# Attention and a bilinear feed-forward layer on one core: empty slots before the late units, wider 128-token steps, a longer run of three weight pieces

## The chip, the core and the metric

The kernel runs on one core of a Trainium2 chip. A core has five engines with an instruction queue each: TensorE (PE, matmuls, with weight loads that overlap them, PEld), VectorE (DVE), ScalarE (ACT), GpSimd (POOL) and SyncE (SP). Here nearly all DMA transfers are issued by SP. Each engine executes its queue in order and waits on semaphores for the others. PE writes to PSUM, which holds eight banks; DVE and ACT read it, POOL does not use it in this kernel. The metric is the device time of one execution in microseconds (us).

## The reference

```python
# q, k, v: (8 batches, 8 heads, 576 rows, 64), tau = 0.02
scores = q @ k.T / 8
thresh = max(scores, axis=-1) - tau
scores = where(scores >= thresh, scores, -1e9)
attn   = exp(scores - max(scores)); attn /= sum(attn) + 1e-9
x      = (attn @ v), heads put side by side        # (4608 tokens, 512)
out    = ((x @ w_a) * (x @ w_b)) @ w_out           # d_ff = 1536, out (4608, 512)
```

The three weight matrices come in as float64 and are turned to float32 on the chip, piece by piece.

## The kernel before, in words

**Units and slots.** Two heads make a pair; 8 batches of 4 pairs are 32 pairs. 576 rows of a head are four times 128 rows and a rest of 64. A unit `(p, u)` is 128 query rows of pair `p`: `u` = 0 to 3 are the full blocks, `u` = 4 (`NT`) joins the rests of two pairs. The list `units` holds 16 units of batch 0 without its rests, then 18 of each other batch, and at its end (from index `late` = 142) two late units for the rests of batch 0, written as pairs 32 and 34. One loop goes over slots `g`; slot `g` issues the scores of unit `g`, the transposes and the swap of unit `g - 1`, the way back of unit `g - 2` and the product with v of unit `g - 3` (`PV_LAG` = 3). Before, there are 144 units and 147 slots.

**The path of a unit.** PE makes the scores into two PSUM buffers (L400). DVE takes the maximum (L407), ACT the exponential (L428), DVE masks and sums (L431) and inverts the sums (L442, L444), ACT scales (L450). For the first units PE transposes the weights (L475, `turn_pe`). Later ones go a longer way: DVE transposes 32 by 32 blocks (L496, `turn_blocks`), SP writes them to DRAM (`swap<-tw`), and SP reads them back rearranged (`wT<-swap`, `turn_back`). Then PE multiplies with v (L540), ACT and DVE copy the result into an x tile (L547, L548), and POOL makes a second copy with the halves exchanged (L563).

**The feed-forward blocks.** 256 tokens form a block: two per batch, and two made of the rests. Layer 1 multiplies x by w_a and w_b and multiplies the two results; layer 2 multiplies by w_out. Most blocks use a scheme with seven products in place of eight (`sevens_of`, L708, with sums by POOL), with some plain steps between (`plain`, L782, evicted by ACT at L788 and by DVE at L790). Layer 2 is L839, or L885 for the very first block, which runs before the sums of w_out exist. The two blocks of batch 0 have all of layer 1 plain, and part of it in steps of 128 tokens: four of six column tiles of the first block, all six of the second. A step has a 128-column tile `f` of one weight group (two tiles make a group), a token range, and both matrices in turn, and each of these takes one PSUM buffer. There are four such buffers (`banks`) of two banks for scores, products and steps together.

**What sets the order.** The program order is written out by this Python loop, and each engine keeps it. `advance(cols)` issues feed-forward matmuls until `cols` columns are spent; a slot's share is `pace`, at most 0.1 of a block's 36864 columns plus a constant 576, and no more than what lets the backlog last to the next block's arrival (`arrivals`). `plain` yields without work while the weights that it needs are not yet converted (`state["converted"]`); the rest of that slot's share is then dropped. `make_room` moves a product to the middle of a step.

**Weights.** 36 pieces of 128x512 are loaded by SP (`load_weights`) and converted with two operations each on ACT (L300, L301), POOL (L307, L326) and DVE (L313, L321). `early[g]` says which pieces start in slot `g`; they end in slot `g + 1`. The slots 0 to 3 take two pieces, 4 to 9 three, 10 to 14 two.

**Transfers.** Late in the kernel transfers are not issued at once but posted in a list (`post`) and issued at a pace, each behind the matmul that PE had reached in program order (`pump`, `passed`). The moves of the swap go ahead of others posted lately. `flush` issues all up to a given one without pacing, just before it is needed. For the late units `last_loads` gives the slots that post the k, the query rests (`qt`, eight small transfers each) and the v, and `last_preps` the slots in which DVE transposes k and qt (`prep`, L366). After the last slot `state["over"]` is set, and the blocks that are left run on, with element-wise work on DVE in place of POOL.

Of the kernel before, what the change touches and what calls it, by code (L numbers as in the profile page):

```python
# [22 lines left out]
PV_LAG = 3  # L23
BY_PE = 8
# [12 lines left out]
SEVENS = 2  # L37
# [17 lines left out]
def kernel(  # L55
# [38 lines left out]
    nc = tc.nc  # L94
    B, H, S, D = q.shape
    P = 128
# [3 lines left out]
    HP = H // 2  # L100
# [655 lines left out]
    def ffn(xT, what):  # L756
# [6 lines left out]
        n = CH // P  # L763
        steps = [(f, 0, HALF) for f in range(NG * n)]
        if kind == "first":
            by = (2 if h == 0 else NG) * n
            steps = [(f, c, c + P) for c in (0, P) for f in range(by)] + steps[by:]
        def plain(steps):
            for f, c0, c1, both in steps:
                while (state["converted"] < 2 * HP * (f // n + 1)  # L770
                       or kind == "first" and rows_of[h] * P < c1):
                    yield 0, 0, 0
                fs = f % n * P
                ht = hs[f][:, :, c0:c1]
                for w in both:
                    pab = banks(c1 - c0, "pab")
                    for k in range(H):
                        for r in range(2):
                            rows = slice(r * D, (r + 1) * D)
                            moving = (x if k < HP else xs)[rows, k % HP, c0:c1]  # L780
                            for c in range(2):
                                nc.tensor.matmul(pab[c * D:(c + 1) * D, r],  # L782
                                                 w[rows, f // n, k, fs + c * D:fs + (c + 1) * D], moving,
                                                 start=(k == 0), stop=(k == H - 1))
                        if k < H - 1:
                            yield c1 - c0, (H - 1 - k) * (c1 - c0), H * (c1 - c0)
                    if w is wa_sb:
                        nc.scalar.copy(ht, pab)  # L788
                    else:
                        nc.vector.tensor_tensor(ht, ht, pab, op=ALU.mult)  # L790
                    yield c1 - c0, 0, 0

        both = wa_sb, wb_sb
        h_of = [work.tile([P, m * n, 2, HALF], FP32, tag=tag, bufs=1, name="h")
# [184 lines left out]
    arrivals = [BY_PE + HP + PV_LAG] + [g + PV_LAG + 1 for g, (i, u) in enumerate(units)  # L979
                                        if i >= HP and i % HP == HP - 1 and parts(i, u)] + [UNITS + PV_LAG]  # L980
    first = {i: g for g, (i, u) in enumerate(units) if u == 0}
    second = {i: g for g, (i, u) in enumerate(units) if u == 2}
# [22 lines left out]

    n = 0
    for g in range(NPIECES):
        size = min(3 if 4 <= g < 10 else 2, NPIECES - n)
        early[g] = list(range(n, n + size))
        n += size  # L1010
    for g in range(len(units) + PV_LAG):
# [2 lines left out]
        while bulk and bulk[0][1] < g - 1:  # L1014
            pump()
        state["converted"] = state["added"]
        here = g < len(units)
        converting = bool(early.get(g)) or bool(early.get(g - 1))
        back = ()
        if BY_PE + 1 < g <= len(units) + 1:  # L1020
            n = g - PV_LAG
            back = (1 if 2 * BY_PE <= n and parts(*units[n]) else 0,)
            if not back[0]:
                turn_back(*units[g - 2])
        if here:
            i, u = units[g]
# [20 lines left out]
        if g > BY_PE and g <= len(units):  # L1047
            turn_blocks(*units[g - 1])
        if g > BY_PE:
            advance(PORTIONS[0] * pace)  # L1050
# [18 lines left out]
        if g > BY_PE:  # L1069
            n = g - PV_LAG  # L1070
            held = 0.0
            now = parts(*units[n]) if BY_PE <= n < len(units) else []
# [17 lines left out]
            if back and back[0] > 0:  # L1090
                turn_back(*units[g - 2])
        for n in early.get(g, [])[:1]:
            convert_first(n)
# [90 lines left out]
```

## Time and profile before

| | |
|---|---|
| median of 3 runs | 1459.63 us (1456.23 to 1460.97) |
| the profiled execution | 1453.36 us, span 1451.6 us |
| mean granted clock of PE | 0.994 |
| chain that ended last | PE 82%, DVE 7%, DMA 4%, issue 3%, SP's queue 2% |
| PE busy in the first slices of 36 us | 6, 7, 7, 8, 8, 8 tenths, then mostly 9 or more |

The profile is of one execution. A row of a timeline gives start, duration, engine, line, operation, output<-input, the number of instructions merged into it, and in brackets how long the engine was idle before it and what it waited for. "issue" means that the engine waited for nothing that the profile can name. Ends of matmuls are modelled, so a PE that is busy is not PE at its peak. A releaser that had long been done when the wait ended was not the real one; often a transfer was. Slots can be told from the starts of the scores (L400): slot 5 starts at 44.3 us, 10 at 96.5, 15 at 148.1, 18 at 175.8; the scores of the first late unit start at 1269.3 us.

### The profile page before, as it was taken

The numbers are of one execution on the slowest core, as the hardware profiler recorded it, in microseconds if no ns is written. First come the engines' busy times: TensorE is split into PE (matmuls) and PEld (weight loads), VectorE is DVE, ScalarE is ACT, GpSimd is POOL, SyncE is SP. The second block draws the span as 40 slices with busy tenths as digits, with TensorE's granted clock in tenths as the row PEclk, the third lists the DMA queues.
The fourth block names the chain that finished last, engine by engine and source line by source line (L and its number), as shares of the span: only waits on it lengthen the run. The fifth ranks groups of instructions, "written<-read, shape, count | busy, mean of one in ns | idle before, by whom it ended". The sixth has DMA issues, their size and how long they took to land.

```text
span 1451.6 us, 79189 instructions
## 1 busy us (share of the span) xinstructions
PE 1377.2 (95%) x35264; PEld 1240.9 (85%) x35264; DVE 1015.7 (70%) x2207; ACT 680.8 (47%) x1254; POOL 488.8 (34%) x685
## 2 busy tenths in 40 slices
PE   6778889999999999999999999999999999889998
PEld 4678588988988898989898899799988789789998
DVE  6897876887767877787778675777677777653223
ACT  5775544545455544545454544454545454421110
POOL 2673462424060606051513251424233242306000
PEclk9999999999999999999999999999999999999999
DMA  9976665667657765667566755577556765651000
GB/s 208 240 212 172 167 171 141 162 171 196 176 148 178 181 177 148 179 169 212 152 166 169 188 138 133 147 183 195 152 135 171 188 167 132 177 142 43 4 18 17
DMA packets 338531, 225.87 MB, mean 156 GB/s; under 512 B 182544, under 2 KB 321808, under 8 KB 338192
## 3 DMA queue, kind: packets, MB, share of 16 engines
q1 hardware_dynamic: 335680, 220.23, 59.4%
q8 instruction: 277, 4.54, 1.4%
q10 hardware_dynamic: 2512, 0.59, 0.2%
q14 instruction: 62, 0.51, 0.1%
HBM read 131.07 MB, written 89.65 MB: 152 GB/s over the span
## 4 chain that ended last, share of the span: by engine, by line
PE 82%; DVE 7%; DMA 4%; issue 3%; SPq 2%; ACT 1%; POOL 0%; DVEq 0%; ACTq 0%; POOLq 0%
PE pab L708 26%; PE po L839 20%; PE pab L782 18%; PE pv L540 9%; PE sc L400 9%; DVE mx L407 1%; DVE tw L496 1%; SPq L144 1%; DMA sums_u<-in_k_dram 1%; DVE tw L431 1%; DMA raw<-in_moe_w_a_dram 1%; DMA raw<-in_moe_w_b_dram 0%; SPq L157 0%; DVE low L313 0%; DVE thr L408 0%
## 5 line engine op out<-in xcount | busy, mean ns | idle before, releaser
L450 ACT ACTIVATE tw<-tw,rcp 128x576 f32<-128x576 f32 x272 | 196.1, 768 | 231.2 <-DVE rcp L444 231.2
L407 DVE TENSOR_REDUCE mx<-sc 128x1 f32<-128x576 f32 x288 | 204.4, 750 | 133.5 <-PE sc L400 133.0
L428 ACT ACTIVATE tw<-sc,bias,scalars 128x576 f32<-128x576 f32 x288 | 239.3, 831 | 10.3 <-ACT bias L427 0.2
L674 POOL TENSOR_TENSOR h<-h,u 128x512 f32<-128x512 f32 x28 | 35.1, 1274 | 597.1 <-DVE h L751 387.3
L431 DVE SCALAR_TENSOR_TENSOR tw<-sc,thr,tw 128x576 f32<-128x576 f32 x288 | 220.9, 798 | 9.5 <-ACT tw L428 9.3
L839 PE MATMUL po<-wo_sb,h 64*64 64x256 f32 x3264 | 206.7, 376 | 0.5 <-DVE h L751 0.3
L496 DVE STREAM_TRANSPOSE tw<-tw 128x576 f32<-128x576 f32 x272 | 194.3, 752 | 0.0
L400 PE MATMUL sc<-kT,qT 64*64 64x288 f32 x2048 | 172.9, 407 | 7.8 <-DVE sums L442 5.3
L839 PEld LDWEIGHTS po<-wo_sb,h 64*64 64x64 f32 x3264 | 156.3, 133 | 27.0 <-issue 1.1
L540 PEld LDWEIGHTS pv<-wT,vm 64*64 64x64 f32 x5472 | 162.0, 137 | 19.2 <-issue 13.7
L540 PE MATMUL pv<-wT,vm 64*64 64x160 f32 (+3 forms) x5472 | 171.4, 270 | 6.5 <-issue 6.0
L808 POOL TENSOR_TENSOR h<-h 128x256 f32<-128x256 f32 x177 | 123.9, 732 | 119.7 <-PE po L839 115.1
L839 PE MATMUL po<-sums_u,h 64*64 64x256 f32 x2448 | 151.3, 377 | 2.8 <-DVE h L790 2.8
L839 PEld LDWEIGHTS po<-sums_u,h 64*64 64x64 f32 x2448 | 112.7, 133 | 27.1 <-DVE h L790 5.8
L708 PE MATMUL pab<-xU,wb_sb 64*64 64x128 f32 x4096 | 135.2, 270 | 0.0
L708 PEld LDWEIGHTS pab<-xU,wb_sb 64*64 64x64 f32 x4096 | 130.3, 133 | 1.9
L400 PEld LDWEIGHTS sc<-kT,qT 64*64 64x64 f32 x2048 | 103.8, 133 | 32.2 <-DVE sums L442 5.8
L427 ACT ACTIVATE bias<-mx,scalars 128x1 f32<-128x1 f32 x288 | 82.8, 288 | 65.2 <-DVE mx L407 64.9
L547 ACT COPY xT<-pv 128x128 f32<-128x128 f32 (+1 forms) x72 | 18.2, 253 | 192.6 <-PE pv L540 192.6
L782 PE MATMUL pab<-xS,wb_sb 64*64 64x256 f32 (+1 forms) x1728 | 99.2, 337 | 4.4 <-issue 4.4
L548 DVE COPY xT<-pv 64x128 f32<-64x128 f32 (+1 forms) x144 | 39.4, 274 | 89.3 <-PE pv L540 87.7
L782 PE MATMUL pab<-xS,wa_sb 64*64 64x256 f32 (+1 forms) x1728 | 100.2, 337 | 0.0
(138 smaller groups left out, 2385.1 us busy)
## 6 DMA issues: line engine op xcount, KB each, us to landing
wT<-swap SPq DMA_DIRECT2D x244, 288.0 KB, 3.9
swap<-tw SPq DMA_DIRECT2D x480, 144.0 KB, 3.2
vm<-in_v_dram SPq DMA_DIRECT2D x144, 72.0 KB, 2.5
kT<-in_k_dram SPq DMA_DIRECT2D x128, 72.0 KB, 3.3
swap<-tw SPq DMA_DIRECT2D x128, 72.0 KB, 2.9
wT<-swap SPq DMA_DIRECT2D x56, 144.0 KB, 3.3
out_dram<-kept SPq DMA_DIRECT2D x30, 256.0 KB, 3.6
qT<-in_q_dram SPq DMA_DIRECT2D x112, 40.0 KB, 3.1
```

The lines of the kernel that those rows point to most:

```text
L400: nc.tensor.matmul(sc[m][o * D:(o + 1) * D, c], qT[r, q0:q0 + D], kT[r, c * SH:(c + 1) * SH], start=True, stop=True)
L407: nc.vector.tensor_reduce(mx[:, c], sc[j], axis=AX.XY, op=ALU.max)
L427: nc.scalar.activation(bias[:, j:j + 1], mx[:, j:j + 1], AF.Copy, scale=e_nscale)
L428: nc.scalar.activation(wb[j], sb[j], AF.Exp, bias=bias[:, j:j + 1], scale=e_scale)
L431: nc.vector.scalar_tensor_tensor(out=wv, in0=sb[j], scalar=thr[:, j:j + 1], in1=wv, op0=ALU.is_ge, op1=ALU.mult, accum_out=sums[:, j:j + 1])
L450: nc.scalar.activation(w, w, AF.Copy, scale=rcp[:, j:j + 1])
L496: nc.vector.transpose(w, w)
L540: nc.tensor.matmul(pv[c * D:(c + 1) * D, y], vm[rows, s], wT[y](rows, s), start=(s == 0), stop=(s == NSLOT - 1))
L708: nc.tensor.matmul(out[c * D:(c + 1) * D, r, f * P:(f + 1) * P], w[g][k][rows, w0:w0 + D], moving[k][rows], start=(fresh and k == 0 and f ...
L782: nc.tensor.matmul(pab[c * D:(c + 1) * D, r], w[rows, f // n, k, fs + c * D:fs + (c + 1) * D], moving, start=(k == 0), stop=(k == H - 1))
L808: (nc.vector if state["over"] else nc.gpsimd).tensor_tensor(*a, **kw)
L839: nc.tensor.matmul(po[c * D:(c + 1) * D, r, y], ht[rows, t0:t0 + D], other[rows, f], start=(f == 0), stop=(f == NF // 2 - 1))
```

## The change

There are three parts.

*Empty slots and moved transfers.* Each of the two late units gets an empty slot before it (`None` in `units`), in which no scores, swap or product are issued for a unit; the code that looks at a unit skips it. There are 146 entries and 149 slots. The table of late loads and preparations is shifted: k 0 and 1 are still loaded in slot `late - 4` but transposed one slot later; qt 0 is still loaded in `late - 2` and transposed one later; k 2 and 3 one later; qt 2 is loaded one slot later and transposed two later; v 0 is loaded one slot earlier, v 3 one later.

*Column tiles.* In the steps of 128 tokens both column tiles of a group are done in one step and share a PSUM buffer: for each matrix, tile `f` fills columns 0 to 127 of both banks and tile `f + 1` columns 128 to 255. Only the first matmul of the first tile starts the accumulation. One eviction then takes both tiles. Steps of 256 tokens are as before.

*Weights.* Slots 4 to 12 take three pieces, slot 13 the last one.

```diff
-            by = (2 if h == 0 else NG) * n
-            steps = [(f, c, c + P) for c in (0, P) for f in range(by)] + steps[by:]
+            by = 2 if h == 0 else NG
+            steps = [(f, c, c + P) for c in (0, P) for f in range(0, by * n, n)] + steps[by * n:]
...
-                fs = f % n * P
-                ht = hs[f][:, :, c0:c1]
+                m, cn = HALF // (c1 - c0), c1 - c0
+                late_f = f - (NG - SEVENS) * n
+                ht = h_of[1][:, late_f:late_f + m] if late_f >= 0 else h_of[0][:, f:f + m]
+                ht = ht[:, :, :, c0:c1].rearrange("p f r w -> p r f w")
                 for w in both:
-                    pab = banks(c1 - c0, "pab")
...
+                    pab = banks(m * cn, "pab").rearrange("p r (f w) -> p r f w", f=m)
+                    left = whole = m * H * cn
+                    for fm in range(m):
+                        fs = (f + fm) % n * P
+                        for k in range(H):
...
+                                    nc.tensor.matmul(pab[c * D:(c + 1) * D, r, fm],
+                                                     w[rows, f // n, k, fs + c * D:fs + (c + 1) * D], moving,
+                                                     start=(fm == 0 and k == 0), stop=(fm == m - 1 and k == H - 1),
+                                                     skip_group_check=m > 1)
+                            left -= cn
+                            if left:
+                                yield cn, left, whole
...
-    units += [(p, NT) for p in range(NPR, NPR + HP, 2)]
-    UNITS = len(units)
...
+    for p in range(NPR, NPR + HP, 2):
+        units += [None, (p, NT)]
...
-    last_loads = {late - 4: [("k", 0), ("k", 1)], late - 2: [("k", 2), ("qt", 0)], late - 1: [("k", 3), ("qt", 2)],
-                  late: [("v", 0), ("v", 1)], late + 1: [("v", 2)], late + 2: [("v", 3)]}
-    last_preps = {late - 2: [("k", 0), ("k", 1)], late - 1: [("qt", 0)], late: [("k", 2), ("k", 3), ("qt", 2)]}
+    last_loads = {late - 4: [("k", 0), ("k", 1)], late - 2: [("k", 2), ("qt", 0)], late - 1: [("k", 3), ("v", 0)],
+                  late: [("v", 1), ("qt", 2)], late + 1: [("v", 2)], late + 3: [("v", 3)]}
+    last_preps = {late - 1: [("k", 0), ("k", 1)], late: [("qt", 0)], late + 1: [("k", 2), ("k", 3)], late + 2: [("qt", 2)]}
...
-        size = min(3 if 4 <= g < 10 else 2, NPIECES - n)
+        size = min(3 if 4 <= g < 13 else 2, NPIECES - n)
...
-        here = g < len(units)
+        here = g < len(units) and units[g] is not None
...
-            back = (1 if 2 * BY_PE <= n and parts(*units[n]) else 0,)
-            if not back[0]:
+            back = (1 if 2 * BY_PE <= n and units[n] and parts(*units[n]) else 0,)
+            if not back[0] and units[g - 2]:
                 turn_back(*units[g - 2])
```

More of the change, by code (lines that the diff above doesn't have):

```diff
@@ L772, in plain @@
                     yield 0, 0, 0
-                fs = f % n * P
-                ht = hs[f][:, :, c0:c1]
+                m, cn = HALF // (c1 - c0), c1 - c0
+                late_f = f - (NG - SEVENS) * n
+                ht = h_of[1][:, late_f:late_f + m] if late_f >= 0 else h_of[0][:, f:f + m]
+                ht = ht[:, :, :, c0:c1].rearrange("p f r w -> p r f w")
                 for w in both:
-                    pab = banks(c1 - c0, "pab")
[L777 to L786, printed above, removed]
+                    pab = banks(m * cn, "pab").rearrange("p r (f w) -> p r f w", f=m)
[3 more added lines that the diff above has]
+                        for k in range(H):
+                            for r in range(2):
+                                rows = slice(r * D, (r + 1) * D)
+                                moving = (x if k < HP else xs)[rows, k % HP, c0:c1]
+                                for c in range(2):
+                                    nc.tensor.matmul(pab[c * D:(c + 1) * D, r, fm],
[5 more added lines that the diff above has]
+                                yield cn, left, whole
                     if w is wa_sb:
@@ L790, in plain @@
                         nc.vector.tensor_tensor(ht, ht, pab, op=ALU.mult)
-                    yield c1 - c0, 0, 0
+                    yield cn, 0, 0
         both = wa_sb, wb_sb
@@ L976 @@
     late = len(units)
[L977 to L985 removed]
+    for p in range(NPR, NPR + HP, 2):
+        units += [None, (p, NT)]
+    taken_by = [(g, *unit) for g, unit in enumerate(units) if unit]
+    arrivals = [BY_PE + HP + PV_LAG] + [g + PV_LAG + 1 for g, i, u in taken_by
+                                        if i >= HP and i % HP == HP - 1 and parts(i, u)] + [len(units) + PV_LAG]
+    first = {i: g for g, i, u in taken_by if u == 0}
+    second = {i: g for g, i, u in taken_by if u == 2}
+    last_loads = {late - 4: [("k", 0), ("k", 1)], late - 2: [("k", 2), ("qt", 0)], late - 1: [("k", 3), ("v", 0)],
+                  late: [("v", 1), ("qt", 2)], late + 1: [("v", 2)], late + 3: [("v", 3)]}
+    last_preps = {late - 1: [("k", 0), ("k", 1)], late: [("qt", 0)], late + 1: [("k", 2), ("k", 3)], late + 2: [("qt", 2)]}
     prep_copy(*prep_pe(0, "q"))
@@ L1046 @@
         load_weights(RAWS if g < 6 else RAWS - 1)
-        if g > BY_PE and g <= len(units):
+        if g > BY_PE and g <= len(units) and units[g - 1]:
             turn_blocks(*units[g - 1])
@@ L1071 @@
             held = 0.0
-            now = parts(*units[n]) if BY_PE <= n < len(units) else []
+            now = parts(*units[n]) if BY_PE <= n < len(units) and units[n] else []
             alone = units[n] if BY_PE <= n < 2 * BY_PE else None
@@ L1089 @@
                 running["owed"] -= NSLOT * width(p, h) // 2
-            if back and back[0] > 0:
+            if back and back[0] > 0 and units[g - 2]:
                 turn_back(*units[g - 2])
```

## The prediction

> **What bounds the kernel now.** First the page's busy rows, then a table of stretches that I cut at the stages, to see where TensorE (PE) is not busy.
>
> ```profile
> span 1451.6 us, 79189 instructions
> PE 1377.2 (95%) x35264; PEld 1240.9 (85%) x35264; DVE 1015.7 (70%) x2207; ACT 680.8 (47%) x1254; POOL 488.8 (34%) x685
> ...
> 150.00:174.00 24.00, 20.46 (x338) 9.84 (x337) 20.64 (x43) 12.51 (x25) 11.32 (x13) 0.93 0.74 183
> 174.00:238.00 64.00, 57.70 (x1919) 53.36 (x1912) 45.18 (x97) 29.13 (x58) 26.00 (x16) 1.00 0.62 157
> 238.00:1258.00 1020.00, 1005.13 (x25623) 905.31 (x25623) 762.29 (x1669) 507.87 (x915) 347.95 (x518) 1.00 0.65 167
> 1258.00:1271.00 13.00, 7.15 (x142) 5.58 (x135) 4.23 (x10) 3.55 (x7) 0.00 (x0) 0.92 0.60 147
> 1271.00:1320.00 49.00, 44.03 (x1272) 42.29 (x1268) 21.57 (x50) 11.29 (x25) 6.56 (x8) 0.95 0.46 122
> 1320.00:1447.00 127.00, 125.76 (x3208) 124.33 (x3198) 41.62 (x76) 14.34 (x23) 20.72 (x36) 1.00 0.04 12
> ```
>
> A stretch's row gives its length, the busy time of PE, weight loads, DVE, ACT and POOL, then the granted clock, the DMA share and GB/s. From 238 to 1258 us PE idles 15 us in 1020: the order of its work is fixed and it is the bound. After 1320 it only drains a backlog. What can be won lies before 238 us and in 1258 to 1320 (11 us idle, clock below 1). A stall of PE in either place moves the end by its full length, since the same matmuls follow it. Next the timeline of PE and DVE there:
>
> ```profile
> 1247.64 1.17 PE L400 MATMUL sc<-kT,qT 64*64 64x288 f32 x15
> ...
> 1269.30 2.48 PE L400 MATMUL sc<-kT,qT 64*64 64x288 f32 x15 [5.33 <-DVE sums L442]
> 1271.45 4.09 PE L708 MATMUL pab<-xU,wb_sb 64*64 64x128 f32 x124
> 1282.99 3.51 PE L708 MATMUL pab<-xU,wb_sb 64*64 64x128 f32 x117
> 1306.50 3.81 PE L540 MATMUL pv<-wT,vm 64*64 64x32 f32 x142 [3.66 <-issue]
> 1317.05 2.33 PE L540 MATMUL pv<-wT,vm 64*64 64x32 f32 x142
> ```
> ```profile
> 1268.93 0.31 DVE L366 STREAM_TRANSPOSE qT<-qT 128x128 f32<-128x128 f32 x1 [7.23 <-DMA qT<-in_q_dram]
> ```
>
> The scores of the first late unit (pair 32, the left-over rows of batch 0) waited 5.33 us. DVE sat 7.23 us in front of the transpose of their queries, whose eight transfers SP issued only at 1259.1 and 1265.6. The product of that unit then waited 3.66 us with no named releaser; SP issued its two transfers wT<-swap at 1303.35, so I read it as that round trip. After each wait the same groups run slower (2.48 against 1.17 us, 3.81 against 2.33). In the head:
>
> ```profile
> 149.48 0.74 PE L885 MATMUL po<-wo_sb,h 64*64 64x512 f32 x4
> 152.55 1.86 PE L885 MATMUL po<-wo_sb,h 64*64 64x512 f32 x8 [2.33 <-POOL wo_sb L326]
> 154.17 2.14 PE L540 MATMUL pv<-wT,vm 64*64 64x64 f32 x72
> 164.58 1.23 PE L540 MATMUL pv<-wT,vm 64*64 64x64 f32 x72
> ```
> ```profile
> PE pab L782 <- DVE h L790: 4.3, 4, 1.6
> PE po L885 <- POOL wo_sb L326: 3.4, 2, 2.3
> PE pab L782 <- DVE tw L431: 0.5, 1, 0.5
> ```
>
> The second fence is who PE waited for in 120 to 240 us (total, times, longest): second-layer matmuls waited for weights still being converted, and first-layer matmuls in 128-token steps waited for a PSUM buffer that DVE had not emptied.
>
> **Part 1, the empty slots and the moved transfers.** No matmul is added or removed. Each empty slot holds only feed-forward columns: about 3686 + 576 columns, and 256 columns of L782 cost 0.43 us (64 matmuls of one step, 2048 columns, in 3.45 us), so about 7.2 us per slot that are taken off the final drain (127 us), no new time. Removed, if the waits go: 5.33 + 3.66; and of the slow groups after them: scores 2.48 - 1.17 = 1.31; L708 4.09 - 3.51 x 124/117 = 0.37; product 3.81 - 2.33 = 1.48. Sum 12.15.
> Moved: the transposes of k 0 and 1 go from slot 140 to 141, of qt 0 from 141 to 142, of k 2 and 3 to 143, of qt 2 from 142 to 144. On SP, qt 2 (8 transfers) goes from slot 141 to 142, v 0 (4) from 142 to 141, v 3 (4) from 144 to 145; the rest keep their slot. qt 0 keeps its load slot and its place behind the eight swap and wT issues, so I let it land at 1268.9 again. Its reader now comes after an empty slot: PE was through slot 141 at 1264.0, plus 7.2 is 1271.2, 2.3 us after landing. Behind that transpose on DVE stand the copies of a product and an eviction (L790); PE has four PSUM pairs and product 7 before it needs them, so I cost this wait at nothing; without that cover it is the 2 to 5 us by which DVE is held. The next thing late is qt 2: after 1267.4 SP still has 32 issues (swap 4, wT 6, out 2, k 4, v 8, qt 8) of 0.45 to 0.65 us, ready at 1282 to 1288 plus 1.9 landing, and its scores start at 1264.0 + 7.2 + 8.2 + 7.2 = 1286.6. New stall between 0 and 3.3; I take 1.5, the middle, as pacing on PE can push either way. The late product gets its wT request at the start of a slot instead of its middle, and a slot and a half instead of one: nothing left. Of the last layers more is issued before the loop ends, so some of the 27 additions L808 that DVE does now (455 ns) go to POOL (732 ns): 7.5 us of POOL at most, and PE waited for L808 nowhere in the whole run, so nothing; without that cover, 7.5. Bounds of the part: -12.15 and, if the qt 2 wait repeats the old one with its slow groups (7.0) and the product waits again (5.1), 0. Taken: -10.65.
> [...]
>
> **Part 2, three pieces a slot to slot 12.** The 36 weight pieces end with slot 13 instead of 14, their last adds (L326) in slot 14 instead of 15. Slot 15 (148.1 to 156.4 us) could do only two F steps of layer 2 before it ran out of pieces, and waited. Removed: 2.33 + 1.10 us; slow groups after: product 2.14 - 1.23 = 0.91, the next scores 1.69 us for 13 against 1.15 for 16, so 0.7. Sum 5.0; I keep 0.5 of it, taken -4.5. Bounds 0 and -5.0. Added in slots 10 to 12: per piece DVE 0.68 + 0.42, ACT 0.68 + 0.68, POOL 0.61 + 1.28. From 120 to 150 PE is busy 29.97 of 30, which hides it; without the cover three pieces of 1.1 us on DVE, 3.3. Taken +1. The loads on SP stay: all 36 were issued by 110.5, with the conversions before slot 10 as they were.
> [...]
>
> **Part 3, both column tiles in one step.** Twenty evictions on ACT and twenty on DVE become ten and ten of twice the size:
>
> ```profile
> L790 DVE TENSOR_TENSOR h<-h,pab 128x512 f32<-128x512 f32 x34 | 22.9, 673 | 34.9 <-PE pab L782 34.9
> L790 DVE TENSOR_TENSOR h<-h,pab 128x256 f32<-128x256 f32 x20 | 8.0, 399 | 5.6 <-PE pab L782 5.5
> L788 ACT COPY h<-pab 128x256 f32<-128x256 f32 x20 | 7.3, 367 | 21.8 <-PE pab L782 21.7
> ```
>
> DVE 8.0 - 10 x 0.673 = 1.3 us less, ACT 7.3 - 10 x 0.58 = 1.5 less, both beside PE: nothing. What counts is that a PSUM pair now takes 3.5 us of matmuls instead of 1.75 before PE needs another, so DVE may be late by twice as much. The waits of L782 for a buffer from 101 to 235 us are 0.43, 0.56, 1.16, 0.49, 1.61 and 0.99, 5.24 together; the longest DVE delay there (scores ready at 177, eviction at 181.3) is 4.3 us, which one step plus the rest of the open one covers. Taken -4.0, bounds 0 and -5.24. Against it: an open group holds one of four pairs over the scores, product and transposes of slots 5 to 10. Waits of that kind now: transposes for the copy L548, 0.35 to 1.51; L782 for a score buffer, 0.92 to 1.45. Between 0 and 6 x 1.5 = 9; taken +1.5, as groups already stay open over slot ends before.
>
> **Sum.** -10.65 - 4.5 + 1 - 4.0 + 1.5 = -16.65. The profiled execution took 1453.36 us (span 1451.6 and 1.76 around it), 6.3 below the median of the runs, 1459.63. It would become 1436.7; from the median, which the result is compared with, 1443.0. I say 1443.
>
> **The rivals.** *The tail's waits come back in another place*: the issues behind qt 2 speak for it, the 2.3 us in hand against it; then only the head is left, -6.0: 1453.6. *The head gives nothing*: DVE is busy 9.75 of 10 us around 44 to 54 us and near 8 later, so a PE that waits less may wait elsewhere: 1459.6 - 10.65, 1449. *No change*: both at once, 1459. *Slower*: DVE executes in order, and qt 0, k 3 and qt 2 each block it behind SP's full queue. Each costs a wait like the old (7.0), 21 in all, and the product 5.1: 26.1 against 12.15 now, less 6.0 from the head: 1467.6. It decides once new stalls in the tail exceed 18.2 us. For it: SP issues almost without a gap from 1251.7 to 1278.7; against it: two empty slots give it 14 us more.
>
> **How the numbers follow.** Chances: forecast 0.52 (1435 to 1450), tail lost 0.15, head lost 0.13, no change 0.08, slower 0.12. A measurement of this kernel tells 0.3%, 4.4 us, from nothing. Below 1455.2 lie the forecast, the head-lost case and most of the tail-lost one: 0.76; within 0.3% 0.12; slower 0.12. The range runs from all bounds at their best (12.15 + 5.0 + 5.24 and the 2.8 of evictions, 1434.4) to no change, leaving out the slower case and a little below: 1435 to 1460.
>
> **What would show it.** Right: no wait of scores over 2 us after 1255; the product of the first late unit without a wait; no L885 wait for L326; L782 waits for L790 under 1.2 us before 240; PE's busy time unchanged. Wrong: a DVE wait for qT or kT of 5 us or more with PE stopped beside it, transposes L475 waiting over 1.5 us in slots 5 to 8, or these stalls gone and a span that stays.

## The result, and the profile after

| | median | range | ratio to the kernel before, 95% interval |
|---|---|---|---|
| before | 1457.28 us | 1456.12 to 1460.97 | |
| changed | 1448.15 us | 1446.29 to 1450.88 | 0.9933 [0.9914, 0.9952] |

The change makes the kernel faster by 0.67%, 9.8 us of 1457 by the ratio. The forecast was 1443.0 us. The profiled execution of the changed kernel has a span of 1446.4 us and a time of 1448.15, which is the median itself; that of the kernel before was a short one, 1453.36 against its median of 1457.28. So the two spans differ by only 5.2 us, and stages have to be compared over more kernels than two. All times here are medians; one disturbed execution of 3663.58 us, of the version that the table of stages calls "to 11, loads", is left out. The changed kernel's page, the lines that answer to those shown of before:

```profile
span 1446.4 us, 79185 instructions
...
PE 1380.9 (95%) x35264; PEld 1250.0 (86%) x35264; DVE 1006.6 (70%) x2188; ACT 680.2 (47%) x1243; POOL 496.1 (34%) x695
...
q8 instruction: 278, 4.55, 1.3%
```

PE's work is the same 35264 matmuls. (The last line is needed later.) The table of stretches of the changed kernel, cut as before; columns are the stretch, its length, busy time of PE, weight loads, DVE, ACT and POOL, the granted clock, the DMA share and GB/s:

```profile
120.00:150.00 30.00, 27.27 (x531) 20.14 (x526) 27.70 (x55) 16.77 (x35) 17.61 (x20) 0.94 0.47 112
150.00:174.00 24.00, 23.70 (x548) 19.30 (x544) 18.72 (x40) 12.54 (x23) 8.74 (x10) 1.00 0.81 203
...
1258.00:1271.00 13.00, 12.79 (x354) 10.90 (x350) 7.12 (x14) 5.46 (x9) 0.00 (x0) 1.00 0.52 117
1271.00:1320.00 49.00, 45.95 (x1106) 42.87 (x1102) 20.57 (x46) 10.00 (x21) 15.46 (x25) 0.97 0.51 133
1320.00:1442.00 122.00, 118.94 (x3179) 117.79 (x3171) 35.77 (x70) 14.12 (x24) 17.97 (x30) 1.00 0.04 12
```

In 150 to 174 us PE is busy 23.70 us, before 20.46. In 1258 to 1271 it is busy 12.79, before 7.15. But 120 to 150, where it was busy 29.97, has become 27.27 at a clock of 0.94. The timeline of the tail shows PE's stops there, then DVE's:

```profile
1273.05 0.90 PE L400 MATMUL sc<-kT,qT 64*64 64x288 f32 x4 [0.16 <-issue]
1274.18 1.04 PE L400 MATMUL sc<-kT,qT 64*64 64x288 f32 x10 [0.23 <-issue]
...
1287.74 2.53 PE L540 MATMUL pv<-wT,vm 64*64 64x160 f32 x67 [0.25 <-DMA wT<-swap]
...
1293.14 2.12 PE L400 MATMUL sc<-kT,qT 64*64 64x288 f32 x14 [2.08 <-issue]
...
1309.15 2.31 PE L540 MATMUL pv<-wT,vm 64*64 64x32 f32 x137
```
```profile
1272.64 0.31 DVE L366 STREAM_TRANSPOSE qT<-qT 128x128 f32<-128x128 f32 x1 [6.64 <-DMA qT<-in_q_dram]
...
1292.72 0.31 DVE L366 STREAM_TRANSPOSE qT<-qT 128x128 f32<-128x128 f32 x1 [7.52 <-DMA vm<-in_v_dram]
```

DVE sits in front of the query transposes, for 6.64 and 7.52 us. (The second row names a v transfer; SP issued the eight transfers of qt 2 from 1285.25 to 1290.13.) Before, the first of these waits was 7.23 us, and the second was short:

```profile
1278.43 0.31 DVE L366 STREAM_TRANSPOSE qT<-qT 128x128 f32<-128x128 f32 x1 [0.91 <-DMA qT<-in_q_dram]
```

But the scores of the first late unit are held by only 0.16 and 0.23 us (5.33 before), since an empty slot's work lies in front of them. The second late unit's scores do wait, 2.08 us, and run slowly after it. The product of the first late unit (1309.15) has no wait; before it had 3.66.

### The profile page after: what moved, and what is told of

It reads as the page before. It is cut to its first block, busy times and chain, and to the rows that moved or that the text cites. A ratio compares the mean times of both kernels' runs of the same rounds, so it can differ in the third digit from the quotient of the medians.

```text
span 1446.4 us, 79185 instructions
## 1 busy us (share of the span) xinstructions
PE 1380.9 (95%) x35264; PEld 1250.0 (86%) x35264; DVE 1006.6 (70%) x2188; ACT 680.2 (47%) x1243; POOL 496.1 (34%) x695
## 3 DMA queue, kind: packets, MB, share of 16 engines
q8 instruction: 278, 4.55, 1.3%
## 4 chain that ended last, share of the span: by engine, by line
PE 82%; DMA 7%; DVE 6%; issue 3%; SPq 2%; ACT 1%; DVEq 0%; ACTq 0%
PE pab L708 25%; PE po L846 19%; PE pab L787 18%; PE pv L540 9%; PE sc L400 9%; PE po L892 1%; DMA qT<-in_q_dram 1%; DVE mx L407 1%; DMA raw<-in_moe_w_a_dram 1%; DVE tw L496 1%; DMA sums_u<-in_moe_w_a_dram 1%; DVE tw L431 1%; DMA wT<-swap 1%; DMA swap<-tw 1%; DMA sums_u<-in_k_dram 1%
## 5 line engine op out<-in xcount | busy, mean ns | idle before, releaser
L431 DVE SCALAR_TENSOR_TENSOR tw<-sc,thr,tw 128x576 f32<-128x576 f32 x288 | 220.9, 798 | 9.8 <-ACT tw L428 9.5
L400 PE MATMUL sc<-kT,qT 64*64 64x288 f32 x2048 | 177.8, 407 | 6.6 <-issue 2.9
L400 PEld LDWEIGHTS sc<-kT,qT 64*64 64x64 f32 x2048 | 107.1, 133 | 31.4 <-issue 7.9
L787 PE MATMUL pab<-xT,wa_sb 64*64 64x256 f32 (+1 forms) x1600 | 93.1, 337 | 8.7 <-issue 4.6
```

The source lines that it names most:

```text
L400: nc.tensor.matmul(sc[m][o * D:(o + 1) * D, c], qT[r, q0:q0 + D], kT[r, c * SH:(c + 1) * SH], start=True, stop=True)
L431: nc.vector.scalar_tensor_tensor(out=wv, in0=sb[j], scalar=thr[:, j:j + 1], in1=wv, op0=ALU.is_ge, op1=ALU.mult, accum_out=sums[:, j:j + 1])
L787: nc.tensor.matmul(pab[c * D:(c + 1) * D, r, fm], w[rows, f // n, k, fs + c * D:fs + (c + 1) * D], moving, start=(fm == 0 and k == 0), sto ...
```

## The experiments

All ratios are to the kernel before on the same chip. Four versions, marked with an asterisk below, were measured on another chip than the other experiments, so versions are compared by their ratios. A ratio less 1, times 1457, gives the us quoted. Durations by stage come from fourteen profiles of thirteen kernels (part 2 alone was measured twice). I take a slot's start from its first scores matmul and cut the span at the starts of slots 12, 15, 46 and 141. Between slots 46 and 141 all of them execute the same program.

```
parts / kernel           span   slot 12 at  12-14  15-45  46-140  141-end
none                    1451.6     122.7    25.4   269.7   836.9   196.9
3                       1460.7     124.5    25.9   268.5   841.5   200.3
2                       1458.5     126.3    30.4   267.7   836.8   197.3
2 (second measurement)* 1453.1     118.4    30.9   265.1   841.1   197.6
2+3                     1451.7     121.6    30.2   263.4   837.9   198.6
1                       1443.7     118.5    26.1   269.6   839.8   189.7
1+2*                    1449.8     124.6    31.0   267.4   837.4   189.4
1+3                     1449.4     116.6    25.6   268.4   848.7   190.0
1+2+3, the change       1446.4     116.8    31.1   263.4   844.0   191.1
 qt ahead               1444.8     119.8    30.2   265.8   837.9   191.0
 pieces to 11           1445.0     123.8    29.3   263.2   839.9   188.9
 to 11, loads           1450.7     124.6    30.8   265.8   842.3   187.2
 to 11, loads, order*   1433.5     120.4    27.6   263.4   836.7   185.3
1+3, loads*             1438.6     119.4    25.9   267.2   840.4   185.7
```

Two columns group cleanly by the parts (12 to 14 and 141 to the end), and they are the ones to read. The start of slot 12 and the stretch 46 to 140 vary by 10 and 12 us whatever the parts; the section on the hardware comes back to that. It is why single totals say little here and the tail's column says much.

### Each part alone

Part 1 is the empty slots and the tables of loads and preparations:

```diff
-    units += [(p, NT) for p in range(NPR, NPR + HP, 2)]
+    for p in range(NPR, NPR + HP, 2):
+        units += [None, (p, NT)]
...
-    last_loads = {late - 4: [("k", 0), ("k", 1)], late - 2: [("k", 2), ("qt", 0)], late - 1: [("k", 3), ("qt", 2)],
-                  late: [("v", 0), ("v", 1)], late + 1: [("v", 2)], late + 2: [("v", 3)]}
+    last_loads = {late - 4: [("k", 0), ("k", 1)], late - 2: [("k", 2), ("qt", 0)], late - 1: [("k", 3), ("v", 0)],
+                  late: [("v", 1), ("qt", 2)], late + 1: [("v", 2)], late + 3: [("v", 3)]}
-    last_preps = {late - 2: [("k", 0), ("k", 1)], late - 1: [("qt", 0)], late: [("k", 2), ("k", 3), ("qt", 2)]}
+    last_preps = {late - 1: [("k", 0), ("k", 1)], late: [("qt", 0)], late + 1: [("k", 2), ("k", 3)], late + 2: [("qt", 2)]}
...
```

> Part 1 alone (empty slots and moved transfers; head and steps as before). Theory A, the head parts are worth something in the end: this part alone gives 5 to 7 us of the 9.1 that the whole change gave, since in the changed kernel's profile the stretch from the scores of slot 140 to the end became 5.3 us shorter. Theory B, what the head parts save is lost again in the middle of the run, as it was in the one profile (8.5 us ahead at slot 62, 0 at slot 140): this part alone gives 9 us, all of it. On the middle: this kernel has the program of before up to slot 140. If the stalls between 240 and 1250 us belong to the program, its slot starts follow those of before within 0.3 us up to slot 140; if they are chance of the execution, they differ by some us.

Measured: 1450.15 us, 0.9961 [0.9943, 0.9979], -5.7 us [-8.3, -3.1], as in theory A. The profile's timeline of PE has these stops in the late units:

```profile
1286.33 4.80 PE L540 MATMUL pv<-wT,vm 64*64 64x160 f32 x69 [1.42 <-DMA wT<-swap]
1292.49 1.36 PE L400 MATMUL sc<-kT,qT 64*64 64x288 f32 x14 [0.57 <-issue]
```

The scores hardly wait, but a product between them waited for the way back of the swap, and half its matmuls ran slowly: 69 in 4.80 us, 67 in 2.53 in the changed kernel. What is late next is one or the other. No run has the empty slots without the new tables, so the two are not told apart.

Part 2 is one number:

```diff
-        size = min(3 if 4 <= g < 10 else 2, NPIECES - n)
+        size = min(3 if 4 <= g < 13 else 2, NPIECES - n)
```

> Part 2 alone (three weight pieces a slot to slot 12). Theory A: faster by 1 to 3.5 us (my terms for it were -4.5 and +1), with no wait of the first second layer for converted weights. Theory B: within 1 us of before, because slots 11 to 13 lose to the conversions, or the middle of the run, what slots 15 and 16 win.

Measured: 1460.41 us, 1.0032 [1.0010, 1.0053], +4.7 us [1.5, 7.7]. In its profile it was 4.7 us late already at the start of slot 10, and up to there its program is that of the kernel before. So it was run a second time (below).

Part 3 is the steps that take both column tiles:

```diff
...
-            steps = [(f, c, c + P) for c in (0, P) for f in range(by)] + steps[by:]
+            steps = [(f, c, c + P) for c in (0, P) for f in range(0, by * n, n)] + steps[by * n:]
...
-                    pab = banks(c1 - c0, "pab")
+                    pab = banks(m * cn, "pab").rearrange("p r (f w) -> p r f w", f=m)
...
```

> Part 3 alone (both column tiles in one 128-token step). Theory A: faster by 1 to 2.5 us (my terms were -4.0 and +1.5): no wait of L782-type steps for an L790-type eviction after 170 us, longer waits of the transposes L475 for the copy L548 in slots 5 to 8. Theory B: within 1 us of before.

Measured: 1456.83 us, 1.0006 [0.9988, 1.0024]: nothing that can be told. The three add to about nothing, and yet the whole gives 9.8. That made me look for an interaction.

### The parts in pairs

The edits are those above, two at a time.

> Parts 2 and 3 together, without part 1. The parts alone gave -5.7 (part 1), +4.7 (part 2) and +0.4 us (part 3), 0.6 less than nothing in sum, but all three give -9.1. Theory A (parts 2 and 3 need each other: with wider steps PE has longer work to do beside the three conversions of slots 10 to 12, and its 152 more matmuls done by slot 18 then come without new stalls): the whole less part 1, -9.1 + 5.7 = -3.4, so 1453 us. Theory B (the two simply add, and the gain comes from part 1 meeting one of them): +5.1, so 1461.5 us.

> Parts 1 and 3 together, without part 2. Theory A (part 3 only pays with part 2): as part 1 alone, -5 to -6, 1450 to 1451.5 us. Theory B (parts 1 and 3 pay together, part 2 costs 4.7 wherever it stands): -9.1 - 4.7 = -13.8, 1442.7 us.

> Parts 1 and 2 together, without part 3. So far part 1 gave -5.7 us alone and part 2 +4.7 alone, but with part 3 in both kernels part 2 was worth -3.8 (parts 2 and 3 against part 3) and 0 (all against parts 1 and 3). Theory A (part 2 costs about 4.7 unless part 3's wider steps cover its third conversion): -5.7 + 4.7 = -1.0, so about 1456 us. Theory B (part 2 is worth nothing in itself, what it wins in slot 15 it loses in slots 13 to 16, and its +4.7 alone came from stalls before slot 10, where its program is still the old one): as part 1 alone, -6 to -8, 1449 to 1451 us.

> Part 2 alone, a second time, profile included. In its first profile 3.6 us of its loss stood ahead of slot 10, where its program does not differ from the kernel before. Theory A (chance of an execution, and of a set of runs): slot 10 starts somewhere else within some 4 us, and the time is +0 to +2 of the kernel before. Theory B (belongs to this program, as by where its instructions lie in memory): slot 10 is late by 3 to 6 us again and the time +3 to +6.

Measured: parts 2 and 3 1454.37 us, 0.9980 [0.9962, 0.9999], -2.9 us. Parts 1 and 3 1448.94, 0.9932 [0.9905, 0.9958], -9.9. Parts 1 and 2 1450.08, 0.9956 [0.9935, 0.9977], -6.4. Part 2 alone for the second time 1455.87, 1.0007 [0.9992, 1.0021], +1.0 us. So theory A held for parts 2 and 3 and for the repeat, theory B for parts 1 and 2, and neither for parts 1 and 3.

The last answers the puzzle. The same program started slot 10 at 101.3 us in its first profile and at 97.1 in its second. Its first median was high by chance or by the occasion (the second was taken on another chip), and not through anything that part 2 does there. What is left of an interaction is not steady: parts 2 and 3 together are 6.6 us below the sum of the two alone, but with part 1 in the kernel 0.8 above it. So I read none from these times. With +2.8 for part 2 alone (the mean of 4.7 and 1.0), each part can be had four times as a difference of two kernels:

- part 1: -5.7, -6.4 - 2.8 = -9.2, -9.9 - 0.9 = -10.8, -9.8 + 2.9 = -6.9; mean -8.2 us
- part 2: +2.8, -6.4 + 5.7 = -0.7, -2.9 - 0.9 = -3.8, -9.8 + 9.9 = +0.1; mean -0.4 us
- part 3: +0.9, -9.9 + 5.7 = -4.2, -2.9 - 2.8 = -5.7, -9.8 + 6.4 = -3.4; mean -3.1 us

A single one of these is uncertain by 3 to 5 us, their means by about 2 (my estimate from the intervals). The sum, -11.7, agrees with the measured -9.8 [-12.5, -7.0].

The stage table says the same of part 1 without this noise. From slot 141 to the end the five profiles without part 1 took 196.9 to 200.3 us, mean 198.1. The five with part 1 and its own table of loads took 188.9 to 191.1, mean 189.8. Part 1 is worth 8.3 us, all of it in the tail.

Part 2 costs in slots 12 to 14 more than what it wins right after them. Kernels without it take 25.4 to 26.1 us there, those with it in full 30.2 to 31.1: some 4.8 us more, with the same matmuls. In slots 15 to 45 they win 3.2 (268.7 against 265.5, the means of the five without and the six with part 2 in full). Together that is a loss of 1.6, where the times give -0.4; which of the two signs holds is open.

Part 3's gain I can't place in a stage. The who-waited-for-whom list of 120 to 240 us shows what its waits became. First part 3 alone, then parts 1 and 2 without it:

```profile
PE pab L787 <- issue: 5.4, 6, 2.0
PE po L892 <- POOL wo_sb L326: 3.4, 2, 2.3
```
```profile
PE pab L782 <- DVE h L790: 3.5, 5, 1.1
```

With part 3 no step waits for an eviction on DVE (L797, which was L790), as it did for 4.3 us before. But stops with no named releaser came up in their place, 5.4 us in six. Counting all of PE's stops over 0.2 us in slots 18 to 24, the five profiles without part 3 have 4.3 to 6.2 us, mean 5.3, and the nine with it 4.4 to 7.3, mean 5.4. These waits went, and the time that PE stood still in these slots did not.

### Which transfers are late in the tail

The changed kernel's SP loads k 2 ahead of qt 0 and issues qt 0 in two halves, at 1260.76 and 1267.79 us; qt 2 comes later:

```profile
1260.76 2.78 SPq L157 DMA_DIRECT2D qT<-in_q_dram  x4
...
1267.79 1.84 SPq L157 DMA_DIRECT2D qT<-in_q_dram  x4
...
1285.25 4.88 SPq L157 DMA_DIRECT2D qT<-in_q_dram  x8
```

First test: both qt early.

```diff
-    last_loads = {late - 4: [("k", 0), ("k", 1)], late - 2: [("k", 2), ("qt", 0)], late - 1: [("k", 3), ("v", 0)],
-                  late: [("v", 1), ("qt", 2)], late + 1: [("v", 2)], late + 3: [("v", 3)]}
+    last_loads = {late - 4: [("k", 0), ("k", 1)], late - 2: [("qt", 0), ("k", 2)], late - 1: [("qt", 2), ("k", 3)],
+                  late: [("v", 0), ("v", 1)], late + 1: [("v", 2)], late + 3: [("v", 3)]}
```

> The changed kernel with the left-over queries posted first: qt 0 ahead of k 2 in slot 140, qt 2 ahead of k 3 in slot 141 (instead of slot 142), v 0 and v 1 in slot 142. If DVE waiting for qt 2 behind SP's queue is what stops PE for 2.08 us before the second late scores, at half clock after it (1.7 us more), those go and the whole is 3 to 4 us faster than the changed kernel: some 13 us below before. DVE's wait for qt 0 falls from 6.6 to about 4 us. Rival: the wait moves on to v 0 or v 1 or the way back of the swap, and the time stays with the changed kernel's, 9 us below before.

Measured: 1446.02 us, 0.9924 [0.9902, 0.9946]; the tail takes 191.0 us, the changed kernel's 191.1. DVE no longer waits for a query, and PE waits for something else:

```profile
1287.74 0.46 PE L540 MATMUL pv<-wT,vm 64*64 64x160 f32 x2 [3.46 <-DMA wT<-swap]
1288.79 4.13 PE L540 MATMUL pv<-wT,vm 64*64 64x160 f32 x67 [0.59 <-DMA wT<-swap]
```
```profile
1269.78 4.95 SPq L157 DMA_DIRECT2D qT<-in_q_dram  x8
1274.78 2.60 SPq L157 DMA_DIRECT2D kT<-in_k_dram  x4
1277.48 2.84 SPq L157 DMA_DIRECT2D swap<-tw  x4
```

SP issued qt 2 and k 3, twelve transfers and 7.55 us, ahead of the swap of unit 141. One queue carries both. Counted from the start of slot 141, SP began this swap 23.7 us later and ended its way back at 31.7; in the changed kernel these were 20.8 and 27.9. The rival was right: the wait moved on.

Second test: qt 0 first and k 3 alone in slot `late - 1`, with everything else behind the swap. This was run with the weights as in the next heading, and again with the weights of the kernel before:

```diff
+    last_loads = {late - 4: [("k", 0), ("k", 1)], late - 2: [("qt", 0), ("k", 2)], late - 1: [("k", 3)],
+                  late: [("qt", 2), ("v", 0)], late + 1: [("v", 1), ("v", 2)], late + 3: [("v", 3)]}
```

> As the run before, and the late loads once more moved: qt 0 ahead of k 2 in slot late-2, k 3 alone in late-1, qt 2 and v 0 in late, v 1 and v 2 in late+1, v 3 in late+3. With qt 2 out of slot late-1 SP has four issues, not twelve, ahead of the swap of unit 141. Theory: qt 0 lands by 1264 and the way back of unit 141 no longer waits behind qt 2, so neither DVE's wait for qt 0 nor PE's 3.5 us for wT return; 1.5 to 4 us under the run before. Rival (the queue of SP is full either way, and qt 2 or the swap of the next unit is late instead): within 1 us of the run before.

> Parts 1 and 3 with the late loads as in the best run so far (qt 0 ahead of k 2 in slot late-2, k 3 alone in late-1, qt 2 and v 0 in late, v 1 and v 2 in late+1, v 3 in late+3) and three weight pieces a slot only to slot 9, as before the change. Theory (the loads are worth the 2.5 to 5 us that the tails' lengths and the last job's times say, and part 2 is worth nothing): 2 to 5 us under parts 1 and 3 alone, 1440.5 to 1446 us, and no DVE wait for qT over 4 us. Rival (the low times of the last job's best run were chance): 1447 to 1450.

Measured: 1438.73 us, 0.9881 [0.9838, 0.9924], and 1441.68 us, 0.9907 [0.9884, 0.9930]. (The profile of the first is of its longest execution, 1452.98 us.) Against the same kernels with the change's table (0.9922 and 0.9932) that is some 4 to 6 us, with intervals that overlap. The tails are the better witness: 187.2 and 185.7 us, against 188.9 and 190.0. Counting the version with DVE's new order below, three tails with these loads take 185.3 to 187.2 us, and the five with the change's table 188.9 to 191.1. So both theories held by the tails, where the times alone leave it open. In the second of the two, DVE transposes qt 0 without a wait, 10.7 us after the start of slot 141 (17.3 in the changed kernel), and qt 2 after a short one:

```profile
1263.58 0.27 DVE L366 STREAM_TRANSPOSE qT<-qT 128x128 f32<-128x128 f32 x1
...
1284.59 0.31 DVE L366 STREAM_TRANSPOSE qT<-qT 128x128 f32<-128x128 f32 x1 [3.16 <-DMA qT<-in_q_dram]
```

No PE wait above 1.1 us is left between 1240 and 1330 us in it.

### What the third weight piece costs

In the changed kernel a step in slot 12 waits for DVE's masking (L431), and the product of slot 13 waits and then runs slowly. Its timeline of PE, and of DVE beside it:

```profile
125.73 1.09 PE L787 MATMUL pab<-xT,wa_sb 64*64 64x256 f32 x16 [0.95 <-DVE tw L431]
...
136.07 2.14 PE L540 MATMUL pv<-wT,vm 64*64 64x64 f32 x70 [1.78 <-issue]
```
```profile
132.48 0.68 DVE L313 SCALAR_TENSOR_TENSOR low<-sums_u,low 128x512 uint32<-128x512 uint32 x1
133.09 0.83 DVE L321 TENSOR_SCALAR wo_sb<-wo_sb 128x512 uint32<-128x512 uint32 x1
133.84 1.42 DVE L496 STREAM_TRANSPOSE tw<-tw 128x576 f32<-128x576 f32 x2
135.19 0.77 DVE L431 SCALAR_TENSOR_TENSOR tw<-sc,thr,tw 128x576 f32<-128x576 f32 x1
135.89 0.08 DVE L431 DVE_READ_ACCUMULATOR tw<-sc,thr,tw 128x1 f32 x1
```

The product starts 0.10 us after DVE has masked the first half of the scores (L431, done at 135.97). The masking is what frees the scores' PSUM buffer. So I read the wait as one for DVE, which had conversions (L313, L321) in front. The same pair, masking then product, stands in part 2 alone (137.51 and 137.61 in its second profile, a wait of 1.77 us). First test: a third piece only to slot 11.

```diff
-        size = min(3 if 4 <= g < 13 else 2, NPIECES - n)
+        size = min(3 if 4 <= g < 12 else 2, NPIECES - n)
```

> All three parts, but three weight pieces a slot only to slot 11, so that slot 12 and 13 convert two each; the pieces still end with slot 13. Theory: the third conversion in slot 12 is what makes DVE late at 131 to 137 us, so that the product waits 1.78 us for a buffer and runs at half clock for some 3.4 us after it. Then that wait is gone, slot 15 still has weights, and the time is 3 to 3.5 us under the changed kernel: 1444.6 to 1445. Rival (DVE is late there by the slots before, or the lost time comes back in the slots between, where PE waits for DVE anyway): within 1 us of the changed kernel, 1447 to 1449.

Measured: 1446.00 us, 0.9922 [0.9896, 0.9948]. The time lies between the two expectations, and the wait itself refutes the theory: it is there as before.

```profile
143.01 1.42 PE L540 MATMUL pv<-wT,vm 64*64 64x64 f32 x70 [1.76 <-issue]
```
```profile
142.12 0.77 DVE L431 SCALAR_TENSOR_TENSOR tw<-sc,thr,tw 128x576 f32<-128x576 f32 x1
142.83 0.08 DVE L431 DVE_READ_ACCUMULATOR tw<-sc,thr,tw 128x1 f32 x1
```

It is not slot 12's third piece, then. The product again starts 0.10 us after the masking, and DVE works from 123.85 to 144.25 us without a gap, so what slots 10 and 11 left it may count too. Second test, on top of the moved loads: from slot 10 on, the conversion that stood ahead of the masking goes behind it. DVE does the same work, in another order.

```diff
-        convert_rest(g, 0)
+        if g < 10:
+            convert_rest(g, 0)
...
         if here:
             weigh(i, u)
+        if g >= 10:
+            convert_rest(g, 0)
```

> All parts, three pieces a slot to slot 11, the moved late loads, and from slot 10 on the first of a slot's conversions on DVE is put behind the masking of the scores instead of ahead of it. Theory: the product at 137 to 143 us waits 1.8 us because DVE masks the scores late and so frees their buffers late; a conversion less in front (0.68 + 0.68 us and what it displaces, 1.35 in all) takes most of this wait: under 0.6 us, and with it 1 to 3.5 us of the time, 1437 to 1440 us. Rival (DVE has no gap there, so whatever is moved only makes the next item late): the wait shrinks but an eviction or a product copy is late instead, and the time stays at 1440 to 1443.

Measured: 1436.79 us, 0.9885 [0.9861, 0.9908], -16.8 us. The wait is 0.44 us, and the conversion now stands behind the masking:

```profile
137.89 1.40 PE L540 MATMUL pv<-wT,vm 64*64 64x64 f32 x70 [0.44 <-PE pab L787]
```
```profile
137.01 0.77 DVE L431 SCALAR_TENSOR_TENSOR tw<-sc,thr,tw 128x576 f32<-128x576 f32 x1
137.72 0.08 DVE L431 DVE_READ_ACCUMULATOR tw<-sc,thr,tw 128x1 f32 x1
...
138.45 0.68 DVE L313 SCALAR_TENSOR_TENSOR low<-sums_u,low 128x512 uint32<-128x512 uint32 x1
```

The wait in slot 12 (0.94 us in the run without the order) is gone too. Slots 12 to 14 take 27.6 us, against 30.8 and 29.3 in the kernels with the same weights and the old order. Eight profiles with the old order and the longer run of pieces have this wait at 1.76 to 1.78 us, and the one with the new order has 0.44: DVE's order is shown to be the cause. In the time itself nothing of it is seen: the ratio is 0.9885, and 0.9881 in the run without the order, which was made on the other chip. Against the change the two intervals, [0.9861, 0.9908] and [0.9914, 0.9952], do not overlap, though only just, and part 2 alone moved by 3.7 us between two occasions. That this version beats the kernel before is clear; that it beats the change is likely.

## Why the prediction was right or wrong

**The sign, the range and the bound were right.** The time came out 5 us above the forecast of 1443.0 and inside 1435 to 1460. Stops of PE near the two ends do move the end: 8.3 us won in the tail by the traces are 8.2 by the times. The forecast was a sum of -16.65; measured were -9.8 [-12.5, -7.0]. Of the signs that I had named, three came out against me: the second late unit's scores waited 2.08 us (over 2), DVE waited 7.52 us for a query with PE stopped beside it, and a transpose L475 waited 2.2 us in slot 6 (over 1.5).

**Part 1, taken at -10.65, measured at -8.3.** The first late unit's wait went (5.33 to 0.16 and 0.23), its product's wait went (3.66 to none), and the drain took no longer (after the last product 2909 matmuls in 118.1 us, before 3214 in 132.1). Two steps were off. "I let it land at 1268.9 again": qt 0 was ready for its transpose at 1272.6, since SP issued its second half at 1267.79 and not at 1265.58. The 2.3 us I had in hand were used up, and the cover held with 0.4 us of waits. "I take 1.5" for qt 2 was the mis-sized term. The wait itself was 2.08, inside the 0 to 3.3 that I gave. But I counted no slow group behind it, though I had counted three such groups for the old waits. The clock was halved from 1293.4 for 3.4 us, which costs some 1.7: 3.8 instead of 1.5, and 2.3 is about the whole difference. It is not an accident of this one profile. In the four others with this table of loads, the waits at the product of unit 141 and at the second late scores, with 1.7 for the slow group that followed in two of them (69 matmuls of the product in 4.80 and 4.47 us, 2.97 in another), add up to 3.7 to 3.9 us. In the three versions with the loads ordered anew neither of the two waits is left, and the tail is 3.7 us shorter (186.1 against 189.8, the means).

**Part 2, taken at -3.5, measured at -0.4 by the times.** What it removes was right: in the changed kernel no second-layer matmul waits for L326 between 120 and 240 us, and parts 1 and 3 without part 2 still have 3.4 us of it. The step that failed is "Added +1": "From 120 to 150 PE is busy 29.97 of 30, which hides it". A busy PE hid nothing of DVE's work here, as DVE held the buffer that PE needed next (PE stopped 0.95 us at 125.73 and 1.78 at 136.07). The row to read was DVE's own (the third busy time), 25.21 of those 30 us before the change, and its place in line: conversions stand ahead of the masking that frees the scores.

```profile
120.00:150.00 30.00, 29.97 (x619) 25.49 (x611) 25.21 (x56) 21.43 (x43) 13.63 (x19) 0.97 0.52 129
```

The cost is +4.8 us in slots 12 to 14, above even the 3.3 that I gave for the case without cover. In the changed kernel it is made of 0.95 us (a step for L431, 125.73), 1.78 (the product) and about 1.7 of half clock, together 4.4 of the 5.3 by which its slots 12 to 14 exceed the mean without part 2.

**Part 3, taken at -2.5, measured at -3.1 with an uncertainty of 2, and wrong in its steps.** The groups are as foretold (34 evictions of full size have become 44, and the 20 half ones are gone):

```profile
L797 DVE TENSOR_TENSOR h<-h,pab 128x512 f32<-128x512 f32 x44 | 29.6, 673 | 36.5 <-PE pab L787 36.5
```

The waits for an eviction on DVE went too. But "Taken -4.0" was not in slots 18 to 24, where those waits had been: PE's stops there add up to 5.4 us with part 3 and 5.3 without. This is the mechanism of the rival *the head gives nothing*, "a PE that waits less may wait elsewhere", and I had it for DVE only. The +1.5 for the buffer held open was about right:

```profile
PE tp L475 <- DVE xT L548: 4.4, 4, 2.2
```

That list, of 36 to 120 us of the changed kernel, has 4.4 us where before had 2.5, so +1.9, with a longest wait of 2.2 us that my list of signs had put among the wrong ones. Where the 3.1 us of the times lie I can't say; slots 15 to 45 (by 1 to 4 us shorter with part 3) and the slots before 12 are candidates, and both vary by as much.

**The rivals.** *The tail's waits come back* is in part what happened, at the second late unit. *Slower* had its condition half filled: DVE did block twice, 6.64 and 7.52 us. It cost PE 2.5 us of waits, 4.2 with the half clock, where two waits like the old one (7.0 with its slow groups) would be 14, since the empty slots put work in front of whoever needs the transposes. So its threshold of 18.2 us was far.

**Early or late, and the clock.** By the trace, both later (in the change) and earlier (both qt early) gave a tail of 191 us, and 185 to 187 us came from another order on the same queue. Taken for one transfer, early or late decided nothing here, as each early issue was another's late one. The clock: PE ran at half clock (granted 0.50) for 3.41 us from 136.3 us after a stop of 1.78 us, and from 1293.4 after one of 2.08. It had done so before the change too, from 152.7 after the stop of 2.33, and there going by the product's 2.14 us was right; I left the clock out of the new wait all the same.

## What to carry to other kernels

When work is moved onto an engine, ask not whether the bound engine is busy at that time but what it will need from the engine that gets the work, and where in that engine's order it stands: with the conversions ahead of the masking PE waited 1.76 us, with the first of them behind it 0.44. When a wait is removed, price the next one with all that comes with it (the slow clock too), and look for the transfer that shares its queue. When totals vary by more than the effect, cut the traces of several kernels at the same marks and compare only the stage that the change touches.

## What the hardware showed that I had not expected

**PE's stops in the head stand on a grid.** Count PE's matmuls modulo 128. In the changed kernel's trace each of the nine stops of PE over 0.2 us in slots 18 to 24 stands at 54 to 65 of this count, whatever line it is in, and the place drifts slowly down, from 65 at 176.01 us to 54 at 231.62. Between 86 and 122 us five of its six stand at 79, and six of seven in the kernel before. The page lists 278 packets of 4.55 MB for the instruction queue q8 (16.4 KB each), and their times go with the stops. Between 36 and 250 us the two traces have 28 stops over 0.2 us that are called "issue". One is the product of slot 13 in the changed kernel, which waits for the masking; it ends 4.22 us after a packet of q8. The other 27 all end 1.29 to 1.69 us after a packet of q8 has ended. Of the 28 stops with a named releaser only two do; theirs are spread from 0.34 to 7.80 us. What PE waits for in these stops is not shown: the trace names no releaser for them, and no run changed the packets by themselves.

**They go with the head's chance.** Between 40 us and the start of slot 12 the stops at 79 to 86 of that count add up to 13.0 us in the kernel before and 7.9 in the changed one, and slot 12 starts at 122.7 and 116.8. Two profiles do not show that the one makes the other. Whether these stops are also why part 3's waits came back is not tested.

**A stop of the same length may or may not cost the clock.** The 70 matmuls of slot 13's product took 2.14 us after 1.78 us of idleness in the changed kernel, and 1.42 after 1.76 us in the run with pieces to slot 11, where the groups behind it were not slow either (the next product's 70 took 1.26). So the length of one gap did not decide here. The clock records of the two traces, before and changed, show what went with it. Between 40 us and 12 us before the end each stretch at half clock (granted 0.50) lasts 3.41 us, and in each trace their starts are whole multiples of 3.413 us apart: in the changed kernel 78.28, 136.31, 1133.00 and 1293.43 us, which are 17, 292 and 47 of these steps apart, in the kernel before 60.58, 118.61, 152.74, 1268.90 and 1306.45, which are 17, 10, 327 and 11 apart. In the steps just ahead of these nine stretches PE idled 1.78 to 3.41 us in sum, in the 798 other steps at full clock 1.89 at most. The stop of 1.78 us in the changed kernel lay in such a step as a whole. Whether a stop of that length costs 1.7 us more (half of 3.41) can't be told from its length, and what else decides it is not shown: no run moved a stop against these steps.
